# Weighted sums two heads behind, three probability buffers, the squares of v pinned late, and a larger share of two-layer work in the second batch

## The chip, the cores and the metric

The kernel runs on one core of a Trainium2 chip. The metric is the device time of one execution in microseconds. The core has a matmul engine (PE, with its weight loads shown as PEld), a vector engine (DVE), a scalar engine (ACT), a general engine (POOL) and a queue that issues transfers (SP). Each engine works through its own list of instructions strictly in the order in which they stand there.

## The reference

Two parts follow each other. The first is causal attention with a decay: 8 batches of 8 heads, 576 rows each, width 64. The second is a two-layer network on the 4608 rows of the attention's output.

```python
scores = (q @ k.T) / sqrt(64) + decay            # causal, 64 heads of 576 x 576
attn   = exp(scores - rowmax);  attn /= attn.sum(-1)
x      = (attn @ v)                              # laid out as 4608 rows x 512
h      = x @ w_in                                # 512 -> 2048
g      = h * clip(h + 3, 0, 6) / 6
out    = g @ w_out                               # 2048 -> 512
```

## The kernel before

**Units.** The list `VH` sets the order of the attention: 4 pairs of heads of the first batch with their first 256 rows (units 0 to 3), the 8 heads of the first batch with their other rows (units 4 to 11), and then one unit for each of the other 56 heads (units 12 to 67). So batch 1 is units 12 to 19, batch 2 is units 20 to 27, batch 3 is units 28 to 35, and so on. Only units from 12 on are touched by most of the change.

**A unit from 12 on.** `rows(v)` makes the scores of one head in two halves. Each half is a PSUM tile `pn` of two banks from a pool with two buffers, filled by pairs of f32 matmuls (page lines 641 and 644), 12 matmuls for the head. DVE takes the row minima of the negated scores in one custom instruction per row chunk (line 650). ACT makes the exponentials in place (line 658) and casts them to f16 into one of three `ring` buffers (line 675). DVE writes the remainders into the same ring buffer (line 624). A DMA transpose (line 696) moves the half into the tile `pT`. `pT` has two buffers, in a tag PHL that the first batch's tiles use too. `av(v, ph)` then makes the weighted sums, 40 small f16 matmuls (lines 721 to 726) into the single PSUM tile `pav`, from `pT` and the split values `v16`. DVE and ACT normalize and split the result, and `x_move` transposes it by DMA into `xT`, the input of the two-layer work.

**One iteration.** The main loop issues, for unit i: `rows(i)`, steps of the two-layer work in between (`fill`), the move of the sums that the iteration before made, and at its end `av` for unit i - 1. When the last head of a batch has been moved, that batch's two-layer tile (512 rows, and every second time a short tile of 128 rows) goes into the queue from which `fill` takes.

**Two-layer work.** `h_unit` is 12 matmuls `ph` of the first layer (lines 810 to 812), followed by ACT and DVE work on the result (818 to 823). `out_unit` is 48 matmuls `po` of the second layer (865 to 867), which need the whole `gT` of the tile. Their PSUM tiles come from `mm_tile`: two buffers of the pool `ps_m`, and for every third tile the single buffer `tr` of the pool `ps_t`. `fill` gets a share per unit from `F_RATE` in batches 0 and 1, and from `even(h)` afterwards, which spreads what is left over the heads until the next tile.

**The scale of v.** Once per batch, at the eighth head, `v_scale(b + 1)` is started for the next batch: ACT squares the loaded values `vst` (line 382) with a sum per partition into `pm`, PE transposes the sums (`pr_v`, line 390) into the single `tr` buffer, DVE takes the maximum, PE spreads it (`pt_v`, line 198), and small DVE steps make a power of two. `v_split` scales the values with it.

**What sets the order.** The code is recorded in the order of the loop, and a scheduler then orders each engine's list with a timeline model of its own. It takes an instruction early when its model finds the operands ready, so a line in the source does not tell by itself where its instruction stands. Buffers of a tag are handed out in the recorded order.

## Time and profile before

| | us |
|---|---|
| median of 3 runs | 1068.47 (1067.56 to 1068.69) |
| the profiled execution | 1066.19 |
| its span, first to last instruction | 1064.4 |
| PE busy | 1028.3 |
| DVE, ACT, POOL busy | 685.4, 607.3, 398.9 |

The profiled execution took 1.8 us more than its span, and the median of the runs is 2.3 us above the profiled execution. PE's busy time is a modelled one: matmuls overlap, so a group's busy times add up to more than the time they take together, and it is the pitch from one start to the next that tells what a matmul costs. The granted clock is given as a share of full speed.

### The profile page before, as it was taken

To read this page: it belongs to the slowest core of one execution; us is meant where nothing else is said; L and a number is where in the kernel's file an instruction comes from. 1 tells how busy PE (TensorE), PEld (TensorE's weight loads), DVE (VectorE), ACT (ScalarE), POOL (GpSimd) and SP (SyncE) were. 2 spreads that over 40 slices of the span, in tenths; PEclk is the share of its full clock that TensorE was granted. 3 is DMA by queue.
4 is the path that set the end of the run, shared out by engine and by line. 5 is a ranking of instruction groups with operands and counts; after the bars stand their busy time and mean duration, and the time that the engine had idled before them with its cause. 6 is when DMAs were issued, how large, how long until landed. Compare 5 with 4: busy or idle time off the path is not lost.

```text
span 1064.4 us, 20926 instructions
## 1 busy us (share of the span) xinstructions
PE 1028.3 (97%) x7865; PEld 621.9 (58%) x7865; DVE 685.4 (64%) x1903; ACT 607.3 (57%) x1222; POOL 398.9 (37%) x436
## 2 busy tenths in 40 slices
PE   8898999976999999999999999999999999999998
PEld 6677767644555755555555755555555755545545
DVE  7979987767775758865765667665865667504500
ACT  4888757455754667655754567556754566405500
POOL 8745564254444444443333244444424342000000
PEclk8899999987999999999999999999999999999999
DMA  7864337456746664665543574465462553400000
GB/s 234 279 206 145 94 74 159 94 118 131 144 96 129 116 131 83 112 120 146 95 86 74 117 155 85 93 141 131 83 107 57 114 95 74 84 22 21 2 20 30
DMA packets 248417, 114.37 MB, mean 107 GB/s; under 512 B 224788, under 2 KB 226124, under 8 KB 248316
## 3 DMA queue, kind: packets, MB, share of 16 engines
q1 hardware_dynamic: 248316, 113.03, 48.5%
q8 instruction: 62, 1.02, 0.4%
q14 instruction: 39, 0.32, 0.1%
HBM read 47.93 MB, written 9.73 MB: 54 GB/s over the span
## 4 chain that ended last, share of the span: by engine, by line
PE 84%; DVE 5%; DMA 4%; ACT 2%; issue 2%; POOL 1%; SPq 0%; ACTq 0%; POOLq 0%; DVEq 0%
PE po L866 11%; PE po L865 11%; PE po L867 11%; PE ph L810 9%; PE ph L811 9%; PE ph L812 9%; PE pn L641 4%; PE pn L644 4%; DMA pT<-ring 2%; PE pav L725 2%; PE pav L732 2%; PE pav L726 2%; PE pav L724 2%; PE phs L836 1%; PE phs L835 1%
## 5 line engine op out<-in xcount | busy, mean ns | idle before, releaser
L470 POOL TENSOR_SCALAR TK<-ST 64x576 fp32r<-64x576 f32 (+1 forms) x68 | 51.6, 759 | 452.5 <-PE pn L641 420.2
L658 ACT ACTIVATE pn<-pn,MF 128x192 f32<-128x192 f32 (+1 forms) x280 | 135.1, 496 | 135.9 <-DVE MF L650 128.3
L866 PE MATMUL po<-w,gT 128*128 128x512 f16 x560 | 208.8, 380 | 0.0
L865 PE MATMUL po<-w,gT 128*128 128x512 f16 x560 | 208.8, 380 | 0.0
L867 PE MATMUL po<-w,gT 128*128 128x512 f16 x560 | 208.2, 380 | 0.0
L810 PE MATMUL ph<-xT,w 128*128 128x512 f16 (+1 forms) x576 | 200.4, 359 | 5.7 <-DVE r L821 5.6
L811 PE MATMUL ph<-xT,w 128*128 128x512 f16 (+1 forms) x576 | 199.7, 358 | 0.0
L812 PE MATMUL ph<-xT,w 128*128 128x512 f16 (+1 forms) x576 | 198.3, 358 | 0.0
L624 DVE SCALAR_TENSOR_TENSOR ring<-pn,ring 128x128 f16<-128x128 f32 (+1 forms) x392 | 138.1, 386 | 75.4 <-ACT ring L675 74.2
L650 DVE CUSTOM_DVE_ANT_0 pn<-pn,W 128x192 f32<-128x192 f32 x280 | 135.9, 499 | 57.1 <-PE pn L644 54.0
L675 ACT ACTIVATE ring<-pn 128x192 f16<-128x192 f32 (+1 forms) x280 | 115.1, 433 | 36.7 <-DVE ring L624 32.8
L821 DVE SCALAR_TENSOR_TENSOR r<-r,ph 128x512 f32<-128x512 f32 (+1 forms) x144 | 89.4, 622 | 67.6 <-ACT r L818 67.2
L641 PE MATMUL pn<-TK,TQ 68*128 68x192 f32 x336 | 118.3, 371 | 6.8 <-ACT ring L675 6.0
L818 ACT ACTIVATE r<-ph,bias_r,SC 128x512 f32<-128x512 f32 (+1 forms) x144 | 104.3, 729 | 31.2 <-PE ph L812 28.4
L823 DVE TENSOR_TENSOR gT<-r,gT 128x512 f16<-128x512 f32 (+1 forms) x144 | 105.0, 731 | 26.4 <-ACT gT L822 25.2
L644 PE MATMUL pn<-T,T 128*128 128x192 f32 x336 | 106.8, 344 | 0.0
L822 ACT CAST gT<-r 128x512 f16<-128x512 f32 (+1 forms) x144 | 82.0, 571 | 39.6 <-DVE r L821 38.4
L483 POOL TENSOR_TENSOR T<-ST,T 64x576 fp32r<-64x576 f32 (+1 forms) x68 | 100.7, 1481 | 5.1
L480 POOL TENSOR_TENSOR T<-ST,TQ 64x576 fp32r<-64x576 f32 (+2 forms) x68 | 92.6, 1361 | 5.4
L867 PEld LDWEIGHTS <-gT 128*128 128x128 f16 x560 | 54.5, 98 | 64.4 <-issue 5.7
L866 PEld LDWEIGHTS <-gT 128*128 128x128 f16 x560 | 54.6, 98 | 59.5 <-issue 4.2
L811 PEld LDWEIGHTS <-w 128*128 128x128 f16 x576 | 56.5, 98 | 54.8 <-issue 10.6
(156 smaller groups left out, 2003.6 us busy)
## 6 DMA issues: line engine op xcount, KB each, us to landing
ST<-in_qk_dram SPq DMA_DIRECT2D x64, 288.0 KB
out_dram<-o SPq DMA_DIRECT2D x33, 256.0 KB
ring<-in_w_out_dram SPq DMA_DIRECT2D x16, 512.0 KB
vst<-in_vS_dram SPq DMA_DIRECT2D x7, 1040.0 KB
ring<-in_w_in_dram SPq DMA_DIRECT2D x9, 512.0 KB
w<-in_w_in_dram SPq DMA_DIRECT2D x7, 512.0 KB
vst<-in_vS_dram SPq DMA_DIRECT2D x14, 130.0 KB
pT<-ring SPq DMA_TRANSPOSE x112
```

Of the source, the lines that this page charges most:

```text
L624: nc.vector.scalar_tensor_tensor(out_, x, PSC, hi, op0=ALU.mult, op1=ALU.subtract)
L641: nc.tensor.matmul(dst, TQ[i][0:D + 4, qs], TK[i][0:D + 4, a:e], start=True, stop=False)
L644: nc.tensor.matmul(dst, T7[j][:, qs], T1[j][:, a:e], start=False, stop=True)
L650: nc.vector.tensor_tensor_reduce(pn[:r, o:o + kw], pn[:r, o:o + kw], W[:r, 4 * P + r - kw:4 * P + r], -0.125, 3.0e38, ALU.add, ALU.min, ac ...
L658: nc.scalar.activation(x_, x_, AF.Exp, bias=mc[:r, e0 + x:e0 + x + 1], scale=-1.0)
L675: nc.scalar.activation(hl[:r, h0[c]:h0[c] + kw], pp[:r, at[c]:at[c] + kw], AF.Copy, scale=PSC)
L810: nc.tensor.matmul(ph, w1[0][:, cc, fs_], xh, start=(cc == 0), stop=False)
L811: nc.tensor.matmul(ph, w1[0][:, cc, fs_], xl, start=False, stop=False)
L812: d = nc.tensor.matmul(ph, w1[1][:, cc, fs_], xh, start=False, stop=(cc == NCC - 1))
L865: nc.tensor.matmul(po, g[:, 0, fc, ts_], w2[:, fc, 0, c], start=(fc == 0), stop=False)
L866: nc.tensor.matmul(po, g[:, 0, fc, ts_], w2[:, fc, 1, c], start=False, stop=False)
L867: d = nc.tensor.matmul(po, g[:, 1, fc, ts_], w2[:, fc, 0, c], start=False, stop=(fc == NFC - 1))
```

## The change

The sums of a head from unit 12 on are made two iterations after its scores instead of one (`sums(2)` keeps two units waiting in the list `late`; units 0 to 11 stay at one). The tag PHL gets a third buffer for it. `even` counts one head more until the next tile. At the end both waiting units are worked off. The squares of v are cut into five pieces of 512 elements per partition in place of two of 1536 and 1024, they share the scratch buffer `junk`, and for batches from 2 on each is placed after the last exponential that had been recorded then (`exps[-1]`, the first half of the batch's eighth head). `pr_v` sums five columns in place of two. `F_RATE` for batch 1 is 0.6 in place of 0.45.

```diff
-    F_RATE = (0.45, 0.45)
+    F_RATE = (0.45, 0.6)
...
-    cs = p2.tile([NHEAD, 2, S], F32R, tag="PHL", name="cs")
+    cs = p2.tile([NHEAD, 2, S], F32R, tag="PHL", bufs=3, name="cs")
...
     def v_scale(b):
-        pm = p2.tile([P, 2], F32, tag="pm", name=f"vm{b}")
-        vj = p2.tile([P, 3 * H, D], BF16, tag="vj", name=f"vj{b}", bufs=1)
-        for i, t in enumerate(v_parts(b)):
-            x = t.rearrange("p c (h e) -> p (c h) e", e=D + 1)[:, :, 0:D]
-            nc.scalar.activation(
-                vj[:, 0:(3 - i) * H], x, AF.Square, accum_out=pm[:, i:i + 1]
-            )
+        pm = p2.tile([P, NCH], F32, tag="pm", name=f"vm{b}")
+        for c in range(NCH):
+            vj = p2.tile([P, S], BF16, tag="junk", name=f"vj{b}_{c}", bufs=1)
+            with tc.issue_after(exps[-1]) if b > 1 else nullcontext():
+                nc.scalar.activation(
+                    vj[:, 0:H * D].rearrange("p (h e) -> p h e", e=D),
+                    v_chunk(b, c).rearrange("p (h e) -> p h e", e=D + 1)[:, :, 0:D],
+                    AF.Square, accum_out=pm[:, c:c + 1],
+                )
...
-        for i in range(2):
+        for i in range(NCH):
             nc.tensor.matmul(
-                pt[0:1, 0:P], pm[:, i:i + 1], identf, start=(i == 0), stop=(i == 1)
+                pt[0:1, 0:P], pm[:, i:i + 1], identf, start=(i == 0), stop=(i == NCH - 1)
             )
...
     def rows(v):
-        pT = p2.tile([P, 3200], F16, tag="PHL", name=f"pT_{v}")
+        pT = p2.tile([P, 3200], F16, tag="PHL", bufs=3, name=f"pT_{v}")
...
-                nc.scalar.activation(
+                d = nc.scalar.activation(
                     x_, x_, AF.Exp, bias=mc[:r, e0 + x:e0 + x + 1], scale=-1.0
                 )
+            exps.append(d.ins)
...
     def even(h):
-        heads = (1 - h) % H + 1
+        heads = (2 - h) % H + 1
...
-    prev = None
+    late = []
+
+    def sums(lag):
+        if not late:
+            return None
+        if VH[late[0][0]][0] == "F" and len(late) < lag:
+            return None
+        w = late.pop(0)
+        av(*w)
+        return w[0] if VH[w[0]][0] == "A" or VH[w[0]][1] % 2 == 1 else None
...
-        if prev is not None:
-            av(*prev)
-            if VH[prev[0]][0] == "A" or VH[prev[0]][1] % 2 == 1:
-                pend_x = prev[0]
+        pend_x = sums(2)
...
-        prev = (i, ph)
+        late.append((i, ph))
     rates[0] = 1.0
-    av(*prev)
-    fill(4)
+    while late:
+        if moved is not None:
+            done(moved)
+            moved = None
+        if pend_x is not None:
+            x_move(pend_x)
+            moved = pend_x
+        pend_x = sums(1)
+        fill(4)
```

The change moves instructions on every engine. Three places matter here. In the rows below a name ends in the unit's number or the batch's, then the half, then a number of the buffer; `pn_27_0` is the first half of the scores of unit 27, `pT_26` the transposed probabilities that the sums of unit 26 read, `po` and `ph` the second and first layer.

PE, around the transposed sums of squares for batch 3 (`pr_v3`). Before, they stand inside the sums of unit 26, and second-layer matmuls lie between them and the scores of unit 28:

```order
L724 MATMUL pav_171<-v16_172,pT_26_3852 128x65
L390 MATMUL pr_v3_4062<-identf_136,vm3_4038 1x128 x2
L725 LDWEIGHTS pT_26_3852
L725 MATMUL pav_171<-v16_172,pT_26_3852 128x64
...
L867 LDWEIGHTS gT_177
L867 MATMUL po_896_0_4091<-w2_176,gT_177 128x512
L641 MATMUL pn_28_0_4185<-TK1_158,TQ1_155 128x192
```

Now four of the five stand right behind the sums of unit 26 and right ahead of the scores of unit 28, with the second layer behind both:

```order
L730 MATMUL pav_171<-v16_172,pT_26_3769 128x65
L392 MATMUL pr_v3_4001<-identf_136,vm3_3970 1x128 x4
L644 MATMUL pn_28_0_4125<-TK1_158,TQ1_155 128x192
...
L647 MATMUL pn_28_0_4125<-T10_160,T70_162 64x64
L392 MATMUL pr_v3_4001<-identf_136,vm3_3970 1x128
L644 MATMUL pn_28_1_4181<-TK1_158,TQ1_155 128x320
...
L647 MATMUL pn_28_1_4181<-T10_160,T70_162 128x448
L869 LDWEIGHTS gT_177
L869 MATMUL po_768_0_4031<-w2_176,gT_177 128x512
```

Between the last score of unit 27 and the first of these four stand now only 3 matmuls `po` and the 40 of unit 26's sums. The 48 matmuls `po_768` that now stand behind were spread around unit 27's scores before.

PE, the same for batch 4, around units 35 to 37. Now:

```order
L730 MATMUL pav_171<-v16_172,pT_34_5247 128x65
L392 MATMUL pr_v4_5487<-identf_136,vm4_5449 1x128 x4
L644 MATMUL pn_36_0_5607<-TK0_157,TQ0_154 128x192
...
L392 MATMUL pr_v4_5487<-identf_136,vm4_5449 1x128
L644 MATMUL pn_36_1_5663<-TK0_157,TQ0_154 128x320
...
L814 MATMUL ph_2_13_0_5502<-xT0_178,w10_174 128x512
...
L725 MATMUL pav_171<-v16_172,pT_35_5416 128x65
...
L644 MATMUL pn_37_0_5770<-TK1_158,TQ1_155 128x192
...
L869 MATMUL po_1344_0_5800<-w2_176,gT_177 128x512
```

Here only unit 34's 40 sums stand between the scores of unit 35 and `pr_v4`, and from there to the scores of unit 37 only one first-layer group (`ph_2_13`, 12 matmuls, which stands after `ph_2_14` and `ph_2_15`) and unit 35's sums. Before, second-layer matmuls of that tile ran through this whole stretch, even between the single matmuls of a unit's scores.

ACT, at the same place for batch 4. Now:

```order
L661 ACTIVATE pn_35_0_5417<-pn_35_0_5417,MF1_170 64x64
L382 ACTIVATE vj4_0_5450,vm4_5449<-vst_173 128x512
L661 ACTIVATE pn_35_1_5493<-pn_35_1_5493,MF1_170 128x448
L679 ACTIVATE ring1_186<-pn_35_0_5417 128x192
L382 ACTIVATE vj4_1_5452,vm4_5449<-vst_173 128x512
L679 ACTIVATE ring2_187<-pn_35_1_5493 128x320
L679 ACTIVATE ring1_186<-pn_35_0_5417 128x576
L382 ACTIVATE vj4_2_5454,vm4_5449<-vst_173 128x512
L679 ACTIVATE ring2_187<-pn_35_1_5493 128x448
L382 ACTIVATE vj4_3_5456,vm4_5449<-vst_173 128x512
L679 ACTIVATE ring1_186<-pn_35_0_5417 64x64
L382 ACTIVATE vj4_4_5458,vm4_5449<-vst_173 128x512
```

The five squares stand among the exponentials and casts of the batch's eighth unit, and four of them ahead of the last cast of its first half. Unit 27 has the same arrangement. Before, the two squares for batch 3 stood among the casts of unit 23, four units earlier.

More of the change, by code (lines that the diff above doesn't have):

```diff
@@ L179, in decay @@
         yield
-        zf = p2.tile([NHEAD, S], F32, tag="PHL", name="zf")
+        zf = p2.tile([NHEAD, S], F32, tag="PHL", bufs=3, name="zf")
         nc.vector.memset(zf, 0.0)
@@ L572, in scores @@
         i, j = v % NQK, v % NL
-        ph = p2.tile([P, 1600], F32, tag="PHL", name=f"pf_{v}")
+        ph = p2.tile([P, 1600], F32, tag="PHL", bufs=3, name=f"pf_{v}")
         def group(dst, k0, q0, q1, m):
@@ L621 @@
     clean = set()
+    exps = []
     def low(out_, x, hi):
@@ L1078 @@
         fill(1)
-        prev = (i, ph)
+        late.append((i, ph))
     rates[0] = 1.0
-    av(*prev)
-    fill(4)
+    while late:
[7 more added lines that the diff above has]
+        fill(4)
     if moved is not None:
         done(moved)
-    x_move(prev[0])
-    done(prev[0])
+    x_move(pend_x)
+    done(pend_x)
     while units:
```

## The prediction

> **What bounds the kernel now.** I read the page first, then PE's waits, then busy time by stretch, then PE's and ACT's timelines around the waits.
>
> ```profile
> span 1064.4 us, 20926 instructions
> PE 1028.3 (97%) x7865; PEld 621.9 (58%) x7865; DVE 685.4 (64%) x1903; ACT 607.3 (57%) x1222; POOL 398.9 (37%) x436
> PE   8898999976999999999999999999999999999998
> PEclk8899999987999999999999999999999999999999
> ```
>
> The reader is to see that PE is the bound, and that its time is missing in two places alone: the start (the first four slices) and slices 9 and 10, where the granted clock falls too. All that a change of order can win lies there; elsewhere PE has no idle time to give, and new idle time is a loss in full. The waits of PE:
>
> ```profile
> PE pav L721 <- DMA pT<-ring: 8.9, 3, 5.3
> PE pn L641 <- ACT ring L675: 6.0, 2, 5.4
> PE ph L810 <- DVE r L821: 5.6, 3, 2.4
> PE pn L641 <- ACT pn L658: 0.6, 1, 0.6
> ```
>
> The sums' wait for transposes is three waits, 8.9 us, of 68 units. So a lag of two removes no recurring cost; it bears on one place. By stretch:
>
> ```profile
> 186.30:212.90 26.60, 26.60 (x209) 16.09 (x207) 18.88 (x62) 12.28 (x31) 6.42 (x8) 0.98 0.47 95
> 212.90:239.50 26.60, 19.92 (x179) 12.27 (x178) 16.34 (x52) 14.43 (x33) 14.35 (x17) 0.81 0.56 118
> 239.50:266.10 26.60, 17.40 (x157) 12.92 (x154) 19.06 (x61) 14.98 (x32) 12.86 (x14) 0.74 0.67 131
> 266.10:292.70 26.60, 26.60 (x200) 14.59 (x199) 21.02 (x55) 20.57 (x41) 11.65 (x12) 1.00 0.71 144
> ```
>
> Columns are time, PE, PEld, DVE, ACT, POOL busy, clock, DMA. From 213 to 266 us PE is idle for 6.68 + 9.20 = 15.9 us, with no engine full. This is the end of batch 1: the first tile of two-layer work is used up, and the next needs unit 19's sums. PE runs on one unit's latency there.
>
> **Squares out of the way (a gain).** Once the squares' wait for their load stopped PE:
>
> ```profile
> 180.96 1.48 ACT L382 ACTIVATE vj<-vst 128x1536 bf16<-128x1536 f32 x1 [3.68 <-DMA vst<-in_vS_dram]
> 183.03 0.42 DVE L821 SCALAR_TENSOR_TENSOR r<-r,ph 128x256 f32<-128x256 f32 x1 [3.13 <-ACT r L818]
> 183.50 0.27 PE L810 MATMUL ph<-xT,w 128*128 128x256 f16 x1 [2.45 <-DVE r L821]
> 180.00:185.00 5.00, 2.55 (x19) 1.89 (x18) 1.37 (x2) 4.04 (x9) 3.90 (x4) 0.87 0.96 203
> 185.00:190.00 5.00, 5.00 (x67) 4.52 (x66) 3.40 (x11) 5.00 (x14) 0.00 (x0) 0.79 0.24 63
> ```
>
> Worth 2.45 us, and 0.13 x 5 + 0.21 x 5 = 1.7 us of clock in the two stretches. The 0.6 us wait on exponentials stands behind another such pair. Sum -4.8 us; the load is issued many units earlier, so the pinned squares never wait for it.
>
> **More transposed sums (a loss).** Five columns in place of two:
>
> ```profile
> L390 PE MATMUL pr_v<-identf,vm x32: 270/271/273, 28.2 to 809.6; 128*1 128x128 f32 x32
> 195.10:195.63 0.53, 0.53 (x4) 1.00 1.13 212
> ```
>
> Two take 0.53 us from start to the next instruction, so three more take 0.8 us. In batches 1 and 3 to 7 PE is full: 6 x 0.8 = +4.8 us. For batches 0 and 2 they fall where PE waits anyway.
>
> **The new place of the squares (the main loss).** PE's list has for unit 27: its scores, 3 `po`, unit 26's sums, four `pr_v3`, unit 28's scores. PE can't pass `pr_v3`, which needs four squares, which stand behind unit 27's own exponentials. First PE's own work:
>
> ```profile
> 209.99:212.00 2.01, 2.00 (x12) 1.00 1.18 159
> 168.30:169.60 1.30, 1.27 (x40) 1.00 0.07 13
> 315.63 0.59 PE L865 MATMUL po<-w,gT 128*128 128x512 f16 x2
> 316.06 0.59 PE L866 MATMUL po<-w,gT 128*128 128x512 f16 x2
> ```
>
> Scores 2.0, sums 1.27, a `po` 0.43 / 2 = 0.215. To the end of the fourth `pr_v3`: 2.0 + 0.65 + 1.27 + 4 x 0.27 = 5.0 us of work. Now the chain from the same start, for a unit whose scores began at 209.99:
>
> ```profile
> 209.99 0.44 PE L641 MATMUL pn<-TK,TQ 68*128 68x192 f32 x1
> 213.25 2.26 ACT L658 ACTIVATE pn<-pn,MF 128x192 f32<-128x192 f32 x5 [6.26 <-DVE MF L650]
> 215.44 0.64 ACT L675 ACTIVATE ring<-pn 128x192 f16<-128x192 f32 x2
> 216.54 1.06 ACT L675 ACTIVATE ring<-pn 128x576 f16<-128x576 f32 x2
> L382 ACT ACTIVATE vj<-vst x14: 1047/1268/1485, 122.1 to 744.3; 128x1536 bf16<-128x1536 f32 x7, 128x1024 bf16<-128x1024 f32 x7
> ```
>
> 3.26 us to the first exponential, 2.2 for the five, 1.9 for the casts (0.64, 1.06, and 0.2 for the 64-row one). A square of 512: 1485 - 1047 ns is the price of 512 elements, 438, so 1047 - 438 = 609 ns; four 2.4 us. Then 0.5 for the last remainder, after which the half's PSUM buffer is free for unit 28's scores. Sum 10.3 us. PE idles 10.3 - 5.0 = 5.3 us. Bounds: starts of scores that followed each other with little between:
>
> ```profile
> 220.65 0.44 PE L641 MATMUL pn<-TK,TQ 68*128 68x192 f32 x1
> 231.87 0.50 PE L641 MATMUL pn<-TK,TQ 68*128 68x192 f32 x1 [5.42 <-ACT ring L675]
> 240.55 0.33 PE L641 MATMUL pn<-TK,TQ 68*128 68x192 f32 x1 [0.55 <-ACT ring L675]
> 247.73 0.23 PE L721 MATMUL pav<-v,pT 128*128 128x65 f16 x1 [5.29 <-DMA pT<-ring]
> 255.97 0.24 PE L721 MATMUL pav<-v,pT 128*128 128x65 f16 x1 [2.42 <-DMA pT<-ring]
> 258.14 0.62 PE L810 MATMUL ph<-xT,w 128*128 128x512 f16 x1
> ```
>
> They lie 8.7 and 11.2 us apart without squares: idle 3.7 to 6.2. I take 5.3, from the chain. The cover that is gone is the second layer: `po_768` waits for the single `tr` buffer, which `pr_v3` holds, so 10 us of ready work stands behind.
>
> Unit 35 is worse. Work to the fourth `pr_v4` is 4.3 us, so idle 10.3 - 4.3 = 6.0 (4.4 to 6.9). Then unit 36's scores 2.0, a `pr_v4` 0.27, `ph_2_13` 12 x 0.215 = 2.6, which brings it to 15.2. Unit 35's sums need both halves transposed: from scores to sums 240.55 to 255.97 is 15.4, 231.87 to 247.73 is 15.9; with squares 0 to 2.4 more. I take 15.9: idle 0.7, and sums to 17.2. Unit 37's scores come 8.7 us after unit 36's, at 19.0: idle 1.8. Together 8.5 us, bounds 4.4 and 11.5. The second layer can't start because `ph_2_13` sat behind `pr_v4` for `tr`. In batches 4, 5 and 6 (units 43, 51, 59) 18 or more first- or second-layer matmuls stand between scores and `pr_v`, several times over, which covers the squares: 0, and 5.3 each if that cover were gone. The squares' extra time on ACT (5 x 0.61 against 1.48 + 1.06, and three more reads of 0.19) is 1.1 us a batch on an engine that is busy 57%.
>
> Clock, for such idle time:
>
> ```profile
> 225.00:230.00 5.00, 1.41 (x40) 1.28 (x40) 3.33 (x7) 3.31 (x8) 4.17 (x4) 0.81 0.02 5
> 230.00:235.00 5.00, 3.13 (x13) 2.75 (x13) 3.25 (x11) 0.76 (x2) 0.09 (x1) 0.50 0.54 103
> 235.00:240.00 5.00, 5.00 (x50) 2.59 (x49) 3.12 (x12) 4.10 (x10) 4.72 (x6) 0.67 0.88 184
> ```
>
> After a gap of 5.4 us the clock was 0.81, 0.50 and 0.67: (0.19 + 0.50 + 0.33) x 5 = 5.1 us at most, part of it in waits; after the gap of 2.45 it was 1.7. I take 2 us for each place, range 0 to 5. The Trainium skill, page "TensorE: Matmul & The Clock Gate", section "HAM oscillation — how this bites in real kernels", says that only idle gaps over about 3.4 us drop the clock; the 2.45 us gap that was followed by 0.87 and 0.79 speaks against it. By that rule the gaps at unit 27, cut up by the `pr_v3`, would cost no clock, and the sum below would be 2 us less.
>
> Unit 27: +7.3 us (3.7 to 11.2). Unit 35: +10.5 (4.4 to 16.5).
>
> **The end of batch 1.** The lag was to remove the waits of 8.9 us here. But the list has after unit 18's scores: unit 17's sums, unit 19's scores, unit 18's sums, unit 20's scores, unit 19's sums, and at once the first layer that needs them moved. The sums are one head behind as before, since the scheduler took them early. From unit 18's scores to the next tile's first layer it was 258.14 - 220.65 = 37.5 us. Now: 8.7 to 11.2 to unit 19's scores, 15.9 to its sums with up to 3 for the five squares, then moving, by unit 17's sums and the first layer that reads them:
>
> ```profile
> 225.04 0.20 PE L721 MATMUL pav<-v,pT 128*128 128x65 f16 x1 [1.16 <-DMA pT<-ring]
> 235.00 0.65 PE L810 MATMUL ph<-xT,w 128*128 128x512 f16 x1
> ```
>
> That is 10.0 us at most, since unit 19's scores ended there; I take 9.5. Together 34 to 39.6. Unit 20's sums and unit 21's scores (3.3 us), which filled waits before, come after it; 15 first-layer matmuls (3.2 us) fill waits instead. I take -2, and -8 (both kinds of wait gone) to +5.
>
> **The rest.** The larger share moves tile 0's work later into batch 1, where PE is full: 0. In the first batch the two-layer work starts about a unit later in PE's list; DVE is near full there, so I bound it at -4 to +4 and take 0. The third buffer costs nothing. The moves of the sums, two transposes a pair of heads, stand a unit later in SP's list; outside batch 1 the first layer that needs them has a whole earlier tile ahead of it, so 0 while such work is left, and a 10 us wait as in batch 1 where it is not. At the end PE's list is the same from the last tile on.
>
> **Sum.** -4.8 + 4.8 + 7.3 + 10.5 - 2 = +15.8 against 1066.19, so 1082.0; with the 2.3 us by which the median stands above the profiled execution, 1084. The lower ends give -4.8 + 4.8 + 3.7 + 4.4 - 8 - 4 = -3.9, the upper ones +4.8 - 4.8 + 11.2 + 16.5 + 5 + 4 = +36.7.
>
> **Rivals.**
>
> *The lag pays and the pins do not hurt* (faster, 0.15). In this case the sums at the end of batch 1 no longer wait: -8.9, with the squares' -4.8 and part of the slow clock (26.6 x 0.19 + 26.6 x 0.26 = 12 us in two slices, a third of it won). The holes at units 27 and 35 stay at some 2 us each and the 4.8 for `pr_v` remains: -8.9 - 4.8 - 4 + 4 + 4.8 = -8.9, 1060. For it speaks the waits' list; against it the order of PE's list in both places, which no timing can change.
>
> *Losses and gains cancel* (0.07): the low ends of both holes without clock, and -8 at the end of batch 1. 1068.
>
> *A longer hole at batch 1's end* (slower yet, 0.18): `pr_v2` stands between unit 18's sums and unit 20's scores, and the moved sums of unit 19 have nothing to cover them, so the stage grows by 5 instead of falling by 2, and each hole loses 5 us of clock: 1084 + 7 + 6 = 1097. It decides from the point where the half clock meets the score matmuls of units 19 and 20: at 231.87 to 235.00 they took 3.1 us against 2.0.
>
> *The change does not do what it says*: in part this is in the forecast, since the lag is not seen in PE's list before unit 27. From unit 36 on it is, where no sum waits in the trace: worth 0.
>
> **How the numbers follow.** The forecast has 0.60, the three rivals 0.15, 0.07 and 0.18. A measurement of this kernel tells about 0.2%, 2.1 us, from no change. Faster 0.15; same 0.07; slower 0.60 + 0.18 = 0.78. The forecast's own range takes the bounds of the two holes alone, 9.7 below and 9.9 above: 1074 to 1094. The range for 8 in 10 leaves out most of the faster rival and half of the slowest: 1066 to 1097.
>
> **What would show it.** The squares: no wait of ACT's L382 line on `vst`, no 2.45 us wait before 190. The holes: PE waits on ACT's squares at `pr_v` in two places, each with 4 us or more in pieces, near 330 and 435, and a clock below 1.00 in those slices; then a wait of `ph` or `po` on the `tr` buffer's side. Batch 1: slices near 9 and 10 still below full. Wrong I am if PE's waits outside slices 1 to 10 sum to under 5 us: then the scores' chain is shorter than the one at 209.99.

## The result, and the profile after

The changed kernel is slower: 1098.11 us median of four runs (1097.44 to 1098.36) against 1068.58 for the kernel before on the same chip (1067.56 to 1069.52), a ratio of 1.0289 with an interval of 1.0267 to 1.0312. That is 1 us above the predicted range (1066 to 1097) and 14 us above the forecast (1084). The direction was right, the size was not.

The page of the changed kernel, its span, PE's busy time and the two rows of 40 slices:

```profile
span 1096.5 us, 21081 instructions
PE 1050.4 (96%) x7913; PEld 628.6 (57%) x7913; DVE 684.8 (62%) x1903; ACT 611.5 (56%) x1270; POOL 394.4 (36%) x436
PE   8879999986998999899999999999999999999998
PEclk7979999988999899899999999999999999999999
```

The 24 more columns of `pr_v`, two instructions each, show in the count (7913 against 7865). New dips stand at the 13th slice of PE's row and the 14th of the clock's (unit 27), and at the 17th of both (unit 35). At the first and third slice the clock is lower than before. PE's waits:

```profile
PE ph L814 <- DMA xT<-xhl: 10.2, 2, 9.1
PE pr_v L392 <- ACT vj L382: 6.1, 7, 1.4
PE pav L736 <- DVE xf L760: 4.3, 3, 2.1
PE pav L725 <- DMA pT<-ring: 2.2, 3, 1.6
```

The wait of the sums for transposes fell from 8.9 to 2.2 us, and one wait of 9.1 us for the moved sums of batch 1 took its place. The 6.1 us behind the squares are new.

To see where the 32 us between the two profiled spans came from, the span is taken apart into three things: PE's idle time, the clock's loss (half of PE's busy time in stretches where the record of the granted clock says half speed), and what is left, PE's work at full clock. The sum of the first two is called the loss of a stretch below. Idle time is read from the view by stretch, here the changed kernel and then the kernel before (columns as in the prediction):

```profile
0.00:110.00 110.00, 94.91 (x563) 69.32 (x563) 83.02 (x231) 74.86 (x161) 66.77 (x89) 0.86 0.71 209
110.00:200.00 90.00, 87.09 (x722) 66.36 (x721) 78.86 (x213) 64.44 (x143) 47.22 (x49) 0.98 0.36 89
200.00:300.00 100.00, 86.19 (x701) 50.70 (x699) 70.84 (x211) 58.80 (x129) 44.60 (x48) 0.91 0.56 119
300.00:400.00 100.00, 95.28 (x838) 59.17 (x835) 60.57 (x187) 52.31 (x121) 39.09 (x43) 0.95 0.52 111
400.00:500.00 100.00, 96.08 (x676) 53.41 (x674) 70.91 (x204) 61.20 (x131) 40.72 (x43) 0.95 0.63 123
```

```profile
0.00:110.00 110.00, 97.06 (x644) 74.77 (x644) 92.48 (x264) 82.53 (x173) 70.84 (x96) 0.92 0.68 213
110.00:200.00 90.00, 87.54 (x702) 64.34 (x702) 72.25 (x207) 60.25 (x130) 43.64 (x45) 0.98 0.47 105
200.00:300.00 100.00, 84.12 (x697) 51.39 (x695) 72.22 (x210) 60.30 (x128) 49.22 (x52) 0.88 0.61 121
300.00:400.00 100.00, 100.00 (x879) 61.41 (x878) 61.64 (x187) 56.45 (x120) 40.27 (x43) 1.00 0.64 125
400.00:500.00 100.00, 99.35 (x735) 54.72 (x733) 70.53 (x205) 58.43 (x118) 40.66 (x42) 1.00 0.56 109
```

The table gives idle time plus clock loss by stretch, and the work, for both kernels and for every experiment below, each from its own profile (us; the two kernels were profiled a second time as experiments 13 and 14). The stretch to 110 us is the start, 200 to 300 the end of batch 1, 300 to 400 holds unit 27, 400 to 500 unit 35. Idle time after 500 us is 4.2 us in the kernel before and between 4.2 and 7.0 in the others, with no clock loss there. A profile is one execution: that of experiment 7 was the slowest of its twelve runs (1069.49 against a median of 1064.14), that of 17 the fastest and that of 18 the slowest of six, so their rows are to be read with care.

| kernel | to 110 | 110-200 | 200-300 | 300-400 | 400-500 | work |
|---|---|---|---|---|---|---|
| before | 20.5 | 4.2 | 23.4 | 0 | 0.7 | 1011.5 |
| before, again (14) | 26.5 | 2.3 | 23.2 | 0 | 0.3 | 1011.1 |
| changed | 29.3 | 4.6 | 17.8 | 9.2 | 8.8 | 1021.3 |
| changed, again (13) | 30.4 | 4.3 | 17.8 | 9.2 | 8.8 | 1019.8 |
| 1 batch 0's five squares alone | 26.3 | 6.6 | 21.7 | 1.4 | 0.3 | 1013.3 |
| 2 changed, batch 0 in two | 23.4 | 0 | 24.3 | 0.8 | 10.4 | 1018.2 |
| 3 changed, no pin | 29.1 | 4.5 | 21.7 | 0 | 0 | 1018.4 |
| 4 pins without lag | 29.3 | 7.7 | 17.9 | 0.7 | 0.7 | 1018.0 |
| 5 pins a unit earlier | 23.5 | 0 | 25.5 | 0 | 4.5 | 1018.5 |
| 6 lag, one column | 23.3 | 0.9 | 24.0 | 0 | 0 | 1010.3 |
| 7 pins, one column, no lag | 27.2 | 5.5 | 23.1 | 0 | 0 | 1007.8 |
| 8 share alone | 20.7 | 6.7 | 29.8 | 0 | 0.1 | 1011.4 |
| 9 as 6, old share | 23.9 | 1.8 | 23.6 | 0 | 0.9 | 1010.7 |
| 10 one column, no lag | 23.9 | 2.5 | 26.1 | 1.1 | 0.2 | 1010.7 |
| 11 changed, old share | 22.4 | 5.4 | 17.4 | 6.2 | 9.0 | 1020.0 |
| 12 as 2, two buffers for `pr_v` | 23.9 | 0 | 23.1 | 9.0 | 2.7 | 1019.0 |
| 15 lag, five columns, no pin | 23.3 | 0.1 | 33.7 | 1.7 | 1.2 | 1016.4 |
| 16 first layer held back | 20.8 | 8.4 | 18.3 | 0 | 0.3 | 1011.8 |
| 17 three squares, early list | 26.5 | 6.2 | 22.0 | 0 | 0 | 1010.6 |
| 18 three squares, late list | 28.9 | 10.4 | 25.2 | 0 | 0.3 | 1012.0 |

### The profile page after: what moved, and what is told of

Its sections match the earlier page's. It is cut to its first block, busy times and chain, and to the rows that moved or that the text cites. A ratio compares the mean times of both kernels' runs of the same rounds, so it can differ in the third digit from the quotient of the medians.

```text
span 1096.5 us, 21081 instructions
## 1 busy us (share of the span) xinstructions
PE 1050.4 (96%) x7913; PEld 628.6 (57%) x7913; DVE 684.8 (62%) x1903; ACT 611.5 (56%) x1270; POOL 394.4 (36%) x436
## 4 chain that ended last, share of the span: by engine, by line
PE 83%; DVE 8%; DMA 3%; ACT 3%; issue 2%; SPq 0%; ACTq 0%; DVEq 0%
PE po L869 11%; PE po L870 11%; PE po L871 11%; PE ph L814 9%; PE ph L815 9%; PE ph L816 9%; PE pn L644 4%; PE pn L647 4%; DMA ring<-in_w_out_dram 2%; DVE pn L653 1%; PE pav L729 1%; PE pav L728 1%; PE pav L730 1%; PE phs L841 1%; PE phs L839 1%
## 5 line engine op out<-in xcount | busy, mean ns | idle before, releaser
L814 PE MATMUL ph<-xT,w 128*128 128x512 f16 (+1 forms) x576 | 203.8, 361 | 10.7 <-DMA xT<-xhl 10.2
L815 PE MATMUL ph<-xT,w 128*128 128x512 f16 (+1 forms) x576 | 203.4, 360 | 0.0
L816 PE MATMUL ph<-xT,w 128*128 128x512 f16 (+1 forms) x576 | 202.9, 360 | 0.0
L827 DVE TENSOR_TENSOR gT<-r,gT 128x512 f16<-128x512 f32 (+1 forms) x144 | 105.9, 737 | 29.6 <-ACT gT L826 28.9
L647 PE MATMUL pn<-T,T 128*128 128x192 f32 x336 | 104.4, 338 | 0.0
L879 ACT ACTIVATE o<-po,SC 128x512 f32<-128x512 f32 (+1 forms) x37 | 24.7, 673 | 132.2 <-PE po L871 130.5
L871 PEld LDWEIGHTS <-gT 128*128 128x128 f16 x560 | 54.7, 98 | 66.1 <-issue 4.6
```

What stands on the lines that cost most here:

```text
L647: nc.tensor.matmul(dst, T7[j][:, qs], T1[j][:, a:e], start=False, stop=True)
L814: nc.tensor.matmul(ph, w1[0][:, cc, fs_], xh, start=(cc == 0), stop=False)
L815: nc.tensor.matmul(ph, w1[0][:, cc, fs_], xl, start=False, stop=False)
L816: d = nc.tensor.matmul(ph, w1[1][:, cc, fs_], xh, start=False, stop=(cc == NCC - 1))
L871: d = nc.tensor.matmul(po, g[:, 1, fc, ts_], w2[:, fc, 0, c], start=False, stop=(fc == NFC - 1))
```

## Experiments

The theory to be tested: the loss has three parts, a late start from the five squares of batch 0, two holes (stretches in which PE idles and then runs at half clock) from pinned squares with too little work beside them, and the columns of `pr_v`; the lag itself is worth little. Below, "no pin" means `nullcontext()` in place of `issue_after(exps[-1])`. Ratios are against the kernel before on the same chip; on the chips of these runs its median was 1064.8 to 1068.6 us.

### The start: batch 0's five squares

Experiment 1 is the kernel before with the new `v_scale` for batch 0 alone; experiment 2 is the changed kernel with the old one for batch 0 (its squares go into the buffer `vst`, and not into `vj`; experiments 5 to 7, 9, 10, 12 and 15 do the same). The cut is shortened:

```diff
+    def v_scale(b):                      # experiment 1: b > 0, experiment 2: b == 0
+        return v_scale_old(b) if b == 0 else v_scale_new(b)
```

> The kernel before with one change: the squares of batch 0 alone in five pieces (five instructions of ScalarE, five matmuls of pr_v0); later batches stay with two. If these five pieces are what makes the start of the changed kernel late (theory: PE's list then has the first first-layer matmuls behind pn_8 where before they stood ahead of ps_6), the first 110 us lose as they did in the changed kernel, idle +2.2 and clock +6.7 = +8.8 us against 1068.6: 1075 to 1079 us, with PE idle and half clock near 70 to 84 us. If the lag or the third buffer made the start late (rival), this kernel is within 0.2% of before, 1067 to 1071 us.

> The changed kernel with one thing put back: the squares of batch 0 in two pieces (written into v's free buffer), all else as changed. Theory: the start's +8.8 us goes, 1098.1 - 8.8 = 1089 us; and since PE's list now has 27 second-layer matmuls ahead of pr_v3 instead of 3 ahead of it, the hole at unit 27 may shrink by up to 5 us: 1084 to 1090 us. Rival (the lag and the later moves make the start late): 1096 to 1099 us.

Experiment 1: ratio 1.0095 (1.0069 to 1.0121), some 10 us. Experiment 2: 1.0172 (1.0147 to 1.0197), 18 us where the changed kernel has 31 (29 to 33). Experiment 1 says that the five squares, with their three more columns, cost some 10 us, and that no lag is needed for it. Experiment 2 gains 13 us on the changed kernel, but by its row of the table not all of that is the start's. Up to 200 us it loses 10.5 us less, at unit 27 8.4 less, and at the end of batch 1 6.5 more. The hole at unit 27 has gone although the pins and the lag are still there: PE's list there has 27 second-layer matmuls ahead of `pr_v3` in place of 3. So an edit in the first batch also moves cover at a place more than 200 us later. The rows of the start and of the stretch after it, of 1 and then of 2, which has the row of unit 27 too:

```profile
0.00:110.00 110.00, 96.51 (x584) 70.96 (x585) 86.01 (x244) 78.04 (x167) 67.41 (x93) 0.88 0.68 209
110.00:200.00 90.00, 85.07 (x716) 64.85 (x714) 76.02 (x208) 64.11 (x137) 45.82 (x46) 0.98 0.41 101
```

```profile
0.00:110.00 110.00, 96.55 (x631) 75.24 (x631) 92.18 (x264) 82.35 (x173) 71.06 (x96) 0.91 0.69 213
110.00:200.00 90.00, 90.00 (x761) 66.47 (x761) 69.70 (x204) 59.94 (x135) 44.75 (x47) 1.00 0.43 105
300.00:400.00 100.00, 99.19 (x904) 62.23 (x903) 63.67 (x195) 56.62 (x129) 43.70 (x47) 1.00 0.61 125
```

With five squares PE and DVE get through fewer instructions by 110 us (584 and 244 against 631 and 264). The count alone is no proof: the second profile of the kernel before, below, has 599 and 253. From 110 to 200 us PE has no idle time at all in experiment 2: the gain of the cut squares is there, 4.2 us as predicted, once the start is not late. In the changed kernel another wait was the longest of that stretch:

```profile
119.62 0.22 PE L528 MATMUL ptm<-identr,MC 128*3 128x128 f32 x1 [1.63 <-DVE MC L519]
```

How can three more squares do that? PE's list is different from unit 5 on: the weights' low parts `low_8` and `low_9` stand in unit 7 where they stood in unit 6, and no first-layer matmul stands ahead of unit 8's scores, where 22.5 (counted in columns of 512) did; by unit 12 it is 84 against 130. Two experiments ask whether this list is the cause. Experiment 16 holds back only the first layer:

```diff
-        while credit[0] >= 1 and units:
+        while credit[0] >= 1 and units and now[0] >= 7:     # now[0] is the unit
```

> The kernel before with one thing changed: the two-layer work of tile 0 isn't handed out before unit 7, so that PE's list has 11 matmuls of 512 columns ahead of unit 8's scores and 24 ahead of unit 9's, where before it had 22.5 and 36 and the changed kernel 0 and 24. The squares are as before. Theory (the late list makes the start late, since PE has less to do in units 6 to 9): idle plus half-clock loss in the first 110 us rises by 3 to 8 us, +3 to +8 us against before on the same chip. Rival (the five squares' own time makes it late, the list doesn't matter): within 2 us of before.

Ratio 1.0008 (0.9995 to 1.0021): no change. The start is as before, 4 us more are lost from 110 to 200 us, and 5 us come back at the end of batch 1. The theory fails as it was put: the place of the first layer alone isn't it. Experiments 17 and 18 take three squares each, in two cuts that give ACT the same work and PE different lists:

```diff
-        for i, t in enumerate(v_parts(b)):
+        for i, t in enumerate(chunks of 3, 1, 1):     # in words; 17; experiment 18: 2, 1, 2
```

> The kernel before with batch 0's squares in three pieces of 3, 1 and 1 chunks. PE's list has the weights' low_8 to low_11 ahead of and around unit 7's scores as before, 12 matmuls of the first layer (in columns of 512) by unit 8's scores, 36 by unit 9's, 127 by unit 12's. If the list decides: within 2 us of before on the same chip. If ScalarE's extra time decides (one square more, some 0.3 us): the same, and equal to the other kernel with three pieces.

> The kernel before with batch 0's squares in three pieces of 2, 1 and 2 chunks: ScalarE's work is that of the kernel with 3, 1 and 1, but PE's list is the late one, low_8 to low_11 in unit 7, no first-layer matmul by unit 8's scores, 24 by unit 9's, 84 by unit 12's. If the list decides: +4 to +10 us against before on the same chip, with idle plus half-clock loss in the first 110 us at 26 us or more, and waits of PE for VectorE at units 11 and 12. If ScalarE's time decides: within 2 us of the kernel with 3, 1 and 1.

Experiment 17: 1.0063 (1.0041 to 1.0085). Experiment 18: 1.0116 (1.0092 to 1.0140). The late list costs 0.5%, some 6 us, more than the early one at the same work of ACT, in their profiles mostly as clock loss, with the largest part (4.2 us) from 110 to 200 us. But the early list, which was to be within 2 us, lost 7 us itself. So the list decides a part; what the one more square does in the early list isn't settled, since its list isn't that of before either. Both write their squares to `vj` as before, so the shared buffer `junk` isn't needed for such a loss.

Experiments 13 and 14 are the two kernels as they are, for a second profile:

> The changed kernel as it is, for a second profile. If the start's loss is the kernel's own, idle plus half-clock loss in the first 110 us is 27 to 31 us again (before: 20.5). If the clock's part of it is chance, idle is again near 15 us and the half-clock loss anywhere from 5 to 14 us, and the time against before on the same chip is +23 to +30 us.

> The kernel before as it is, for a second profile: idle near 13 us in the first 110 us. If the clock's part is chance, the half-clock loss differs from the first profile's 7.6 us by 2 us or more; the squares' wait of 2.4 us near 183 us is there in both.

Changed: 1.0291 (1.0270 to 1.0312). Before: 0.9993 (0.9977 to 1.0010). The rows of the start, of the changed kernel's second profile and then of the second one of before:

```profile
0.00:110.00 110.00, 95.67 (x566) 70.91 (x566) 80.07 (x233) 75.36 (x162) 65.51 (x89) 0.84 0.69 209
```

```profile
0.00:110.00 110.00, 92.62 (x599) 70.44 (x600) 88.60 (x253) 80.41 (x167) 71.25 (x94) 0.91 0.68 209
```

The changed kernel's start repeats (29.3, 30.4). That of before doesn't (20.5, 26.5), against what was expected of its idle time: 4.4 us of idle time and 1.6 of clock are one execution's own. A better mean comes from all runs: up to unit 11, PE's list is the same in the changed kernel and in experiments 1, 3, 4, 11 and 13, and it is that of before in experiments 2, 5 to 10, 12, 14 and 15. The first six profiles lose 22.4 to 30.4 us by 110 us, 27.8 in the mean, the other eleven 20.5 to 27.2, 23.6 in the mean. The two sets overlap, but their means say that the late list costs some 4 us in the start, where one pair of profiles made it look like 8.8. From 110 to 200 us the six lose 5.5 us in the mean (4.3 to 7.7); of the other list's kernels, the eight with the cut squares in later batches lose 1.4 (0 to 5.5). That makes another 4 us.

### The holes: pinned squares

Unit 27 in the changed kernel, PE's instructions and then ACT's from the last exponentials on:

```profile
352.36 0.38 PE L392 MATMUL pr_v<-identf,vm 128*1 128x128 f32 x2 [1.45 <-ACT vj L382]
353.71 0.58 PE L392 MATMUL pr_v<-identf,vm 128*1 128x128 f32 x2 [0.96 <-ACT vj L382]
355.17 0.59 PE L392 MATMUL pr_v<-identf,vm 128*1 128x128 f32 x2 [0.88 <-ACT vj L382]
356.21 0.59 PE L392 MATMUL pr_v<-identf,vm 128*1 128x128 f32 x2 [0.45 <-ACT vj L382]
356.73 0.53 PE L644 MATMUL pn<-TK,TQ 68*128 68x192 f32 x1
```

```profile
351.59 0.62 ACT L382 ACTIVATE vj<-vst 128x512 bf16<-128x512 f32 x1
...
353.55 0.96 ACT L679 ACTIVATE ring<-pn 128x320 f16<-128x320 f32 x2
354.39 0.63 ACT L382 ACTIVATE vj<-vst 128x512 bf16<-128x512 f32 x1
...
355.43 0.64 ACT L382 ACTIVATE vj<-vst 128x512 bf16<-128x512 f32 x1
```

Unit 27's scores began at 346.66, so unit 28's came 10.1 us later; the chain in the prediction was 10.3. Experiment 3 takes the pin out, experiment 4 puts pins and five squares into the kernel before, without lag:

```diff
-            with tc.issue_after(exps[-1]) if b > 1 else nullcontext():    # experiment 3
+            with nullcontext():
```

> The changed kernel without the pin of the squares behind the last exponentials; lag, third buffer, rate and five pieces stay. Theory (the pinned squares make the holes at units 27 and 35): both holes go, 9.15 + 8.8 = 18 us, the start's +8.8 stays: 1078 to 1083 us, and PE idles under 1 us between 345 and 385 and between 450 and 490 us. Rival (the holes come from the lag: the sums and the layers behind them are late whatever the squares do): 1093 to 1099 us.

> The kernel before with five pinned squares alone: no lag, two buffers, old rate. PE's list has second-layer matmuls between the pr_v matmuls at units 27 and 35. Theory (the pin costs only where the lag has used up the second layer that could stand there): no holes at 27 and 35; start +8.8, pr_v +5.6, squares' wait -2.4 to -4.2: 1078 to 1082 us. Rival (the pin alone makes PE wait for the squares at each batch): two holes of 9 us more, 1094 to 1100 us.

Experiment 3: 1.0135 (1.0112 to 1.0157), 14 us. Experiment 4: 1.0125 (1.0098 to 1.0151), 13 us. The theory holds for both. In experiment 3, without the pin, no idle time and no half clock from 300 to 500 us:

```profile
300.00:400.00 100.00, 100.00 (x880) 61.13 (x879) 67.71 (x209) 56.26 (x122) 45.89 (x48) 1.00 0.56 119
400.00:500.00 100.00, 100.00 (x739) 55.10 (x739) 70.81 (x200) 61.89 (x133) 43.92 (x47) 1.00 0.53 113
```

With pins but no lag (experiment 4), 0.7 us is lost in each stretch; PE's list there has second-layer matmuls between the `pr_v`. So neither the pin nor the lag makes the hole alone: the pinned squares need cover, that is, other work for PE, and in the changed kernel's list it stood elsewhere. Experiment 5 moves the start of `v_scale` one head earlier (batch 0 in two pieces), experiment 12 gives `pr_v` the two-buffer pool:

```diff
-        if b + 1 < B and h == 7:                       # experiment 5
+        if b + 1 < B and h == 6 + (b == 0):
...
-        pt = (ps_m if b == 0 else ps_t).tile(          # experiment 12
+        pt = ps_m.tile(
```

> The changed kernel with batch 0's squares in two pieces and, for later batches, the squares and pr_v started one head earlier (behind the exponentials of the batch's sixth head, not its seventh). In PE's list pr_v3 then stands in unit 26 with some 60 second-layer matmuls around it, pr_v4 in unit 34 behind 24 first-layer matmuls and 40 sums (2.0 + 5.2 + 1.3 + 1.1 us of work, 9.5, against a chain of 10.3). Theory (a hole needs pinned squares with too little work between the scores and pr_v): idle time at both places under 1.5 us each, no half clock there; against before on the same chip start 0 to +3, squares -4, pr_v +6.7: +3 to +7 us. Rival (pinned squares under a lag of two hold PE up wherever they stand): a hole of 9 us moves with them to unit 34 (near 430 us), +12 us or more.

> The changed kernel with batch 0's squares in two pieces and pr_v in the pool of two matmul buffers, not in the single one that the second layer and the ptm tile use too. In PE's list some 22 second-layer matmuls then stand between the pr_v3 matmuls at unit 27, and 12 first-layer matmuls between those of unit 35. Theory (the single buffer kept ready work behind pr_v, as the prediction had it): by PE's work against the chain of 10.3 us the two holes lose 1 to 5 us where the run with the single buffer lost 10.8; against before on the same chip +9 to +14 us. Rival (the buffer doesn't matter, pinned squares do): +18 to +21 us, as with the single buffer.

Experiment 5: 1.0120 (1.0092 to 1.0147). At unit 26, with 48 second-layer matmuls around the squares, PE has no idle time; at unit 34 4.5 us are lost, of which 0.6 is a wait for a square and 1.2 one for transposes. The time is in the rival's range all the same, since the columns (7 us), the end of batch 1 (+2) and the end (+2.8) are in it: the cover held where it was ample, and the sum of the other terms was too low. Experiment 12: 1.0147 (1.0126 to 1.0169), 16 us, between theory and rival. Unit 35 lost 2.7 us in place of the 10.4 of experiment 2. Its list has 12 first-layer matmuls between the `pr_v`, as it should if the `tr` buffer had held them back, but also 40 more sums ahead of them, so the saving isn't the buffer's alone. And at unit 27 the list now has unit 26's sums straight behind the scores, and PE waited 4.7 us for their transposes ahead of `pr_v3`:

```profile
PE pav L747 <- DMA pT<-ring: 4.7, 1, 4.7
```

The two holes together lost 11.7 us, against 11.2 in experiment 2, so the theory, which had 1 to 5, fails on them.

### The share, the lag and the columns

Experiment 8 is the kernel before with `F_RATE = (0.45, 0.6)`; experiment 11 the changed kernel with `(0.45, 0.45)`.

> The kernel before with the larger share of two-layer work in batch 1 alone (0.6 for 0.45). PE's list is the same in the first batch, and pr_v2 stands in unit 18 where it stood in unit 15. Theory (the share costs nothing by itself, as the prediction had it): -4 to +1 us against before on the same chip, the lower end if the squares' wait near 183 us goes with pr_v2's place. Rival (the share uses up the second layer that the end of batch 1 needs): +3 us or more, in slices 9 and 10.

> The changed kernel with batch 1's share of two-layer work back at 0.45, all else as changed. PE's list has the same lines around units 27 and 35, the same late start, and 48 second-layer matmuls between unit 20's scores and unit 21's where the changed kernel has first-layer matmuls of the next tile. Theory (in the changed kernel the share is worth nothing either way: its end of batch 1 took no longer than before): +26 to +31 us against before on the same chip. Rival (the share's 5 us, measured alone, are in the changed kernel's loss): +20 to +25 us.

Experiment 8: 1.0051 (1.0030 to 1.0072), 5 us slower; the theory falls. The end of batch 1 has 29.8 us of loss in place of 23.4, and a wait for the moved sums as in the changed kernel:

```profile
PE ph L810 <- DMA xT<-xhl: 5.1, 1, 5.1
```

PE's list offers a reason, which no run tests by itself. Before: unit 18's scores with 6 first-layer matmuls, unit 17's sums, unit 19's scores, 9 first-layer matmuls, unit 18's sums. With the larger share: unit 18's scores, unit 17's sums, 15 first-layer matmuls, unit 19's scores, unit 18's sums. These are matmuls of the next tile that need only heads that are already moved, 27 in all. The last nine are spent a unit sooner, and nothing covers unit 19's latency. Experiment 11: 1.0214 (1.0190 to 1.0239), 8 us less than the changed kernel. That is 23 us above before, in the rival's range, yet its end of batch 1 is no better (17.4 against 17.8), so neither theory has the reason right: 3 us of the difference are at unit 27, where the list has 13 second-layer matmuls beside the sums in place of 3; 7 are in the start of this one profile, whose list is the changed kernel's own up to unit 11 and whose time was 3.5 us below the median of its runs. So a part of the start's 7 is this execution's chance, and what remains of the 8 stays open.

Experiments 6, 9 and 10 have batch 0's squares in two pieces, no pin, and the columns added by VectorE, so that `pr_v` is one matmul; 6 keeps lag, third buffer and larger share, 9 the lag with the old share, 10 none of them. Experiment 7 is 10 with the pins; experiment 15 is 6 with five columns.

```diff
+        pv = p2.tile([P, 1], F32, tag="pm")
+        nc.vector.tensor_reduce(pv, pm, axis=AX.X, op=ALU.add)
...
-        for i in range(NCH):
-            nc.tensor.matmul(pt[0:1, 0:P], pm[:, i:i + 1], identf, ...)
+        nc.tensor.matmul(pt[0:1, 0:P], pv, identf, start=True, stop=True)
```

> The changed kernel's lag, third buffer and rate, with batch 0's squares in two pieces, no pin, and in later batches the five pieces' columns added by VectorE, so that pr_v is one matmul. It takes out the three losses found (start, holes, columns) and keeps the lag. Theory: PE's work at full clock falls by 8 x 0.28 = 2 us against before, the end of batch 1 stays within 3 us of before: -6 to +1 us against before on the same chip. Rival (the lag has a cost of its own, such as moved sums that come later): +3 us or more, with PE waiting for xT outside the first 110 us.

> The kernel before (no lag, two buffers, old rate) with the pinned squares alone for batches 1 to 7, their five columns added by VectorE, and batch 0 as before. Theory (the pin is a gain where other work covers it): the squares' wait near 183 us goes, -4.2, one column instead of two, -2.2, and the end of batch 1 gives up to 5 us back as in the kernel with pins and no lag: -6 to -12 us against before on the same chip. Rival (the pins cost as much as they give): within 2 us of before or slower.

> The lag, the third buffer, one pr_v column, no pin, batch 0's squares in two pieces, and batch 1's share of two-layer work back at 0.45. Theory (the larger share costs some 5 us by itself, by the run with it alone): -7 to -11 us against before on the same chip. Rival (the share costs only where nothing else is changed, since the order at the end of batch 1 decides): -2 to -6 us, as with 0.6.

> The kernel before with the five pieces for batches 1 to 7 and their columns added by VectorE, no pin, no lag, two buffers, old share. It tells what the lag adds to the kernel with lag and one column. Theory (the lag gives nothing at the end of batch 1, as the prediction had it, and nothing later): one column in place of two, -2.2, and up to -2 for the squares, which now wait in smaller pieces: -1 to -5 us against before on the same chip. Rival (the lag is a gain of 4 us or more): +2 to -1 us.

> The changed kernel without the pin and with batch 0's squares in two pieces: lag, third buffer, larger share and five columns stay. If start, holes and columns are the whole loss, what is left against the kernel with lag and one column (-4.3 us) is 28 columns at 0.28 = 7.8 us: +2 to +5 us against before on the same chip. If a part is missing, it shows as +8 us or more.

| experiment | median us | ratio |
|---|---|---|
| 6 lag, larger share, one column | 1064.34 | 0.9960 (0.9942 to 0.9977) |
| 7 pins, no lag, one column | 1064.14 | 0.9966 (0.9943 to 0.9990) |
| 9 lag, old share, one column | 1066.48 | 0.9989 (0.9972 to 1.0006) |
| 10 no lag, no pin, one column | 1069.24 | 1.0006 (0.9990 to 1.0022) |
| 15 lag, larger share, five columns | 1085.81 | 1.0191 (1.0169 to 1.0213) |

Experiment 6 beats both kernels, by 4 us against before, and its theory holds. Experiment 7 is 4 us faster too, but its theory said 6 to 12. Experiment 10 is no faster than before, against its theory: one column alone gains nothing that can be measured. Experiment 9 fails its theory as well, since the old share is no better there; as the intervals of 6 and 9 overlap, the runs don't show whether 6's gain needs the larger share beside the lag. Nor does the lag do in 6 what it was made for: at the end of batch 1 the sums still wait for transposes,

```profile
PE pav L748 <- DMA pT<-ring: 7.4, 3, 4.4
```

and the stretch loses as much as before (24.0 against 23.4 and 23.2). By the table 6 gains from 110 to 200 us (0.9 against 4.2 and 2.3) and 1 us of work. Experiment 15 was to be +2 to +5 us and is +20: a part was missing. The columns are 6 us of the difference to 6 (work 1016.4 against 1010.3). The other 10 are the end of batch 1, 33.7 against 24.0 us. Experiment 6's list has 6 and 9 first-layer matmuls in units 18 and 19, as before; experiment 15's has all 15 in unit 18, as with the share alone, and the same wait:

```profile
PE ph L838 <- DMA xT<-xhl: 5.8, 2, 4.7
```

So with five columns in place of one at unit 17, nine other matmuls stand a unit earlier, and that costs more than the columns. All profiles whose list has at least six of them, or second-layer matmuls, behind unit 19's scores lose 17.4 to 26.1 us at the end of batch 1; the two lists with none there lose 29.8 and 33.7.

### The clock

In the kernel before, around the gap of 2.45 us, and in the changed one, around unit 27, cut at the points where the granted clock changes:

```profile
180.32:183.73 3.41, 0.96 (x10) 0.70 (x9) 0.70 (x2) 2.77 (x6) 3.19 (x4) 1.00 1.12 241
183.73:187.15 3.42, 3.42 (x37) 2.81 (x35) 1.73 (x4) 3.42 (x8) 0.39 (x1) 0.50 0.31 58
187.15:190.56 3.41, 3.41 (x46) 3.02 (x44) 2.90 (x11) 2.96 (x10) 0.00 (x0) 1.00 0.32 88
```

```profile
350.27:353.68 3.41, 1.02 (x23) 0.60 (x19) 1.26 (x6) 3.38 (x11) 3.19 (x4) 1.00 0.03 7
353.68:357.10 3.42, 2.06 (x8) 0.63 (x8) 2.25 (x6) 3.23 (x10) 0.57 (x1) 0.50 0.34 86
357.10:360.51 3.41, 3.41 (x14) 2.53 (x13) 1.70 (x7) 0.00 (x0) 0.06 (x1) 0.50 0.94 178
360.51:363.92 3.41, 3.41 (x9) 1.24 (x9) 1.57 (x7) 2.90 (x8) 3.20 (x5) 0.50 0.34 65
363.92:367.34 3.42, 3.42 (x17) 1.56 (x16) 2.08 (x6) 1.29 (x3) 2.17 (x2) 1.00 0.04 7
```

In each of the 20 profiles every change of the clock lies on a grid of 3.413 us, within a hundredth of a step; where it lies against the span's start differs: its first point comes 0.20 to 2.87 us later. Taking PE's busy share in each such window at full clock: under 0.45 the next window was at half clock in 76 of 77 cases, from 0.45 to 0.60 in 43 of 72, from 0.60 to 0.75 in 10 of 79, above that in 3 of 5712. At unit 27 no gap was over 1.45 us, and 10.2 us ran at half clock: idle time in pieces drops it as well. Of the windows under 0.45 with no gap over 1.5 us in them, 10 of 11 were followed by half clock, so the share tells more than the longest gap. At half clock, a window with PE busy under 0.75 was always followed by another (104 of 104), one over 0.90 in 54 of 173. The Trainium skill, page "TensorE: Matmul & The Clock Gate", Part 1, speaks of a free-running window of 3413 ns, and the traces agree. The rule that the prediction weighed, that only gaps over about 3.4 us drop the clock, doesn't hold here: no window was without work in the two places above.

## Why the prediction was wrong

The measured side of the table is the mean of the two profiles of each kernel, in us; it adds up to the 30.2 between the spans. The prediction's 0.6 us wait on exponentials lay between 400 and 420 us, so it stands with unit 35:

| term | predicted | measured |
|---|---|---|
| start | 0 (-4 to +4) | +6.4 |
| squares out of the way (110 to 200 us, without the 0.6) | -4.2 | +1.2 |
| work at full clock, `pr_v` and the rest | +4.8 | +9.2 |
| unit 27 | +7.3 | +9.2 |
| unit 35 (+10.5, less the 0.6) | +9.9 | +8.3 |
| end of batch 1 | -2 | -5.5 |
| idle time after 500 us | 0 | +1.5 |

**The step that failed** is "DVE is near full there, so I bound it at -4 to +4 and take 0", on the first batch's two-layer work. The prediction saw the late list and named it, and priced it at nothing because DVE is near full there. Experiment 1 prices it at some 10 us with all that follows, three more columns (0.8 us) included: some 4 us in the start by the means of 17 profiles (6.4 by two of each kernel), and another 4 from 110 to 200 us, which took the squares' gain back (4.6 us lost there in the changed kernel; with the list of before up to unit 11, 0 to 0.1 in experiments 2, 5, 12 and 15, and 0.9 to 5.5 in 6, 7, 9 and 10). DVE's load was no ground for a term of nothing: with the late list it is busy 83.0 us of the first 110, before 92.5, so it wasn't kept full. Why the list costs this much is shown only in part and stays open: by experiments 16 to 18 neither the first layer's place alone nor ACT's work alone accounts for it.

**The pr_v columns** were mis-sized: 24 columns at 0.27 us are 6.5 us, and the prediction counted 4.8, on the ground that those of batches 0 and 2 fall into waits. Experiments 2, 3 and 4, which have the later batches' columns and at most one hole, show 6.9 us more work at full clock. The other 2.3 us of the changed kernel's work appear with both holes and aren't attributed.

**The holes** were right in place and mechanism: the chain from unit 27's scores is 10.1 us against 10.3. That the size came out too, 17.5 us for both against 17.2, is in part luck, since two errors cancel, less idle time and more clock than said: 4.7 and 4.4 at unit 27 (said 5.3 and 2), 3.9 and 4.8 at unit 35 (said 8.5 and 2). At unit 35 the squares held PE up for 2.4 us, and 1.6 were a wait of unit 34's sums for their transposes, which the prediction didn't have:

```profile
456.11 0.24 PE L725 MATMUL pav<-v,pT 128*128 128x65 f16 x1 [1.57 <-DMA pT<-ring]
```

The 2.5 us of idle time that it expected behind `pr_v4` didn't come; from 464 to 468 us PE was busy throughout, at half clock. By the rule of the clock that was weighed, unit 27 would have cost no clock; it cost more than was taken. That the `tr` buffer holds ready work back at unit 35 agrees with experiment 12's list.

**The end of batch 1**: -5.5, inside the bounds of -8 to +5. The idle time fell by 1.9 us, as forecast (2); the other 3.6 are clock loss, of which the term had nothing. The waits for transposes went, and the 9.1 us wait for the moved sums is the one that the prediction described.

**The larger share** was put at 0 because it "moves tile 0's work later into batch 1, where PE is full". Alone it costs 5 us, and by the lists of experiments 8 and 15 it is where nine matmuls end up that costs it, not their number; in the kernel with the lag and one column it costs nothing (experiments 6 and 9).

**What would show it**: no wait of ACT for `vst`'s load and no 2.45 us wait before 190, true; PE's waits on the squares, said near 330 and 435, at 352 and 459, with 3.8 and 2.4 us in pieces where 4 each were said; a wait on the `tr` buffer's side behind them, not seen, since PE had no gap there; the clock under 1.00 there, true; slices near 9 and 10 below full, true. Of the rivals, the longer hole at batch 1's end came near in time, 1097, by luck: its stage got shorter and not longer. Only its 5 us of clock for each hole was right (4.4 and 4.8).

## What to carry to other kernels

When a list's order comes from a scheduler's model, a change in one place can cost most in another where the list moved: compare the lists at every stage that has idle time, and price each shift of cover by the work that leaves the stage. A pin behind late work needs cover that is counted in the list, matmul by matmul, against the chain it waits for. Profile the kernel before twice before a few microseconds of a start are given to a cause.

## What the runs showed that was not expected

In these profiles the clock followed PE's busy share: below 0.45 of a 3.413 us window the next was at half speed in 76 of 77 cases, and at unit 27 no gap was over 1.45 us. The same list up to unit 11 lost between 4.8 and 16.1 us of clock in the first 110 us (experiments 11 and 13), and the kernel before took 1062.0 to 1070.7 us in twelve runs on one chip; the place of the grid alone doesn't explain this, since experiments 3 and 4, with the same list there and grids that lie 0.06 us apart against the span's start, lost 12.6 and 16.1 us, and their idle times differ the other way (16.4 and 13.3). Each square with a sum is followed by a read of the accumulator of 0.2 us on ACT, so five squares pay five of these where two paid two.
